# Six edits to the order of stores, norms and loads in a fused forward and backward kernel: last stores from SyncE, a store behind the first norm's power steps, norms by groups and behind sums, an own tile for a gradient, a table loaded later

## The chip, the core and the metric

The kernel runs on one core of a Trainium2 chip. The core has TensorE (PE) for matrix products, VectorE (DVE), ScalarE (ACT) and GpSimd (POOL) for elementwise work, SyncE (SP), which here does nothing but issue DMA transfers, and 16 DMA engines, which carry the transfers that SP and POOL issue. The five engines run their own instruction streams and meet only at semaphores. The metric is the device time of one execution in microseconds. The kernel before takes 729.11 us, the median of 3 runs (725.36 to 734.2).

## What is computed

A residual stack of four parts over x = A_q, of shape [1, 2048, 448] in bf16: two gated long convolutions (A) and two SiLU MLPs (B), each behind a layernorm without weights; the same weights serve both layers. Both the output and the gradients of seven of the inputs come back.

```python
def _A_ref(q, k, v, shift_k, ssm_k, ssm_D):
    k_shift = sum(k_pad[:, t:t + S, :] * shift_k[:, ks - 1 - t] for t in range(ks))
    kv = k_shift * v
    y = irfft(rfft(kv, 2 * S) * rfft(ssm_k, 2 * S))[:, :S]
    return q * (y + kv * ssm_D)

def _B_ref(x, w1, w2):
    return silu(x @ w1) @ w2          # w1 [448, 1792], w2 [1792, 448]

x = A_q
x = x + _A_ref(ln(x), A_k, A_v, A_shift_k, A_ssm_k, A_ssm_D)
x = x + _B_ref(ln(x), B_w1, B_w2)
x = x + _A_ref(ln(x), A_k, A_v, A_shift_k, A_ssm_k, A_ssm_D)
x = x + _B_ref(ln(x), B_w1, B_w2)
out, vjp = jax.vjp(f, A_q, A_k, A_v, A_shift_k, A_ssm_k, A_ssm_D, B_w1, B_w2)
return (out, *vjp(grad_out))
```

(The reference's lines, shortened: the convolution is written with real FFTs of length 4096.)

## The kernel before

The convolution's result y + kv*D does not depend on x, so a first stage (`_ssm_prefix`, about the first 100 us) computes it once for all tokens as Y (`Ysb`), with the FFT written as matrix products; the spectra of ssm_k and kv go to DRAM for the backward part. What is left of part A in the main stage is a norm and a gate, x + ln(x)*Y.

The main stage (`Main.run`) works on the 2048 tokens in four chunks c of 512, each of four tiles `tl` of 128 tokens. All tokens of the residual stream lie in one tile X in SBUF. For each chunk and layer L there are these steps, each a generator whose yields mark where another may come between:

- `T`, `T2`: TensorE transposes of a normed tile, so that the features lie on the partitions (nT). `T2` works by groups of tiles: 0 and 1, then 2, then 3.
- `H`: h = nT times w1 in seven steps; ACT writes silu(h) into aT (L659) and copies h into dT (L664), which `slope` later turns into the slope of silu (L674).
- `O`: aT times w2, eight steps; for each tile DVE adds the result into X (L685, in the waits "X L685"). In layer 1 the output is stored from X by POOL (L687), once a chunk, after tile 3.
- `G`: the gradient times w2 transposed, seven steps, into ghT, which DVE multiplies by the slope (for c = 0 to 3 of layer 1 in the loop at L845). In layer 1 the gradient that goes in is grad_out, which `load_gT` brings in transposed: eight DMA transposes on SP for a chunk, per tile one of 384 features (L750) and one of the last 128 (L751).
- `N`: ghT times w1 transposed, and the backward of the layernorm (`_ln_bwd`, L894 to L899, whose last addition writes its output with the residual gradient added). In layer 1 `_ln_bwd` runs twice a tile, for norm 3 and for norm 2, and both write into X in place; gb is the residual gradient, loaded by SP.
- `_ln` (L250): a layernorm. DVE takes the statistics, adds the epsilon (L268), POOL raises to the power of -1/2 (L270), DVE makes the shift (L272) and, for each tile, the normed n (L277), which POOL stores into N_d for the backward part of A. It takes `groups` of tiles, and each group is one such sequence. The norms are numbered si = 0 to 3. `fwd0(c)` is norm 0, the gate and norm 1; `fwd1(c)` is norm 2, the gate and norm 3.
- `store`: aT or ghT, transposed by SP's DMA transposes into a tile "turned" (L553), goes on to DRAM (a_d, g_d), from where it is loaded for the weight gradients as dstat.

On TensorE the order is written out by hand: `steps` and `weave` take patterns of letters, and each letter runs one generator up to its next yield. The other engines are ordered by a scheduler, under `issue_after` and priorities where the code sets them. Tiles come from pools with a few buffers for a name; a new use of a buffer waits for the last readers of the old one.

The weight gradients (`Jobs`) are products over all tokens, woven in from the last chunk on: the stationary side is dstat, loaded by SP in 512 KB pieces, the moving side is X, grad_out or the normed inputs (L969). `fin_w2` copies a finished block of w2's gradient to SBUF by ACT (L1054) and POOL stores it (L1056).

The last stage (`_ssm_suffix`, from about 508 us) is the backward part of the convolution. It loads the spectra K and KV again in pieces of 2048 columns (`spec_load`, L1150 and L1151), the normed inputs of part A (q_n, L1092), and a table Minvs of 1 MB for the inverse FFT (`_load_minv`, L200), which its products read first at 639 us. POOL issues all of these. The remaining weight gradients fill TensorE between its steps, and the kernel ends with the blocks 12 and 13 of w2's gradient.

Of the kernel before, what the change touches and what calls it, by code (L numbers as in the profile page):

```python
# [17 lines left out]
P = 128  # L18
S = 2048
D = 448  # L20
# [232 lines left out]
def _ln(k, pool, c, src, si, n_g, groups=((0, 4),), pin=False, eng=None, behind=None):  # L253
    nc = k.nc
    for lo, hi in groups:
# [14 lines left out]
        nc.gpsimd.tensor_tensor(out=r[:, lo:hi], in0=ve[:, 0:n], in1=k.mhalf[:, 0:n], op=ALU.pow)  # L270
# [7 lines left out]
    if si != 2:  # L278
        lo, hi = groups[0][0], groups[-1][1]
        nc.gpsimd.dma_start(out=_pm(k.N_d[si][:])[:, 4 * c + lo:4 * c + hi, :], in_=n_g[:, lo:hi, :])  # L280
# [243 lines left out]
class Main:  # L524
    def __init__(self, k, es):
# [10 lines left out]
        nc.gpsimd.dma_start(out=_pm(k.Y_d[:]), in_=k.Ysb[:])  # L536
# [61 lines left out]
    def a_fwd(self, c, si, src, n_g, groups, behind=None):  # L598
        nc, X = self.nc, self.X
        if len(groups) > 2:  # L600

            for g in groups:
                _ln(self.k, self.ch, c, src, si, n_g, (g,))
                self.gate(c, src, n_g, (g,))
            return
        _ln(self.k, self.ch, c, src, si, n_g, groups, behind=behind)
        self.gate(c, src, n_g)
# [16 lines left out]
    def fwd0(self, c):  # L624
# [51 lines left out]
    def O(self, c, L, aT):  # L676
        nc, k, X = self.nc, self.k, self.X
        for tl in range(4):
# [7 lines left out]
            if L == 1 and tl == 3:  # L686
                nc.gpsimd.dma_start(out=_pm(k.outs[0][0])[:, 4 * c:4 * c + 4, :], in_=X[:, 4 * c:4 * c + 4, :])  # L687
# [26 lines left out]
    def N(self, c, L, gh, gres, n_b, n_a):  # L714
# [4 lines left out]
        for tl in range(4):  # L719
# [3 lines left out]
            Gt = self.X[:, t, :] if L == 1 else g1[:, tl % 2, :]  # L723
            pn = k.psum.tile([P, 512], FP32, name="ps_n", tag="po", bufs=2)
# [6 lines left out]
            _ln_bwd(k, self.ch, u0[:], n_b[:, tl, :], cp[:, tl, :], gres(tl), Gt)  # L731
            if L == 1:
                nc.vector.tensor_tensor(out=gyt[:, tl, :], in0=Gt, in1=n_a[:, tl, :], op=ALU.mult)
                u1 = self.t([P, D], "lb_u1", "lb_u0", 3)
                nc.vector.scalar_tensor_tensor(out=u1[:], in0=Gt, scalar=k.rstd[2][:, t:t + 1], in1=self.Y[:, t, :], op0=ALU.mult, op1=ALU.mult, accum_out=cp[:, 4 + tl, 0:1])
                self.chain = _ln_bwd(k, self.ch, u1[:], n_a[:, tl, :], cp[:, 4 + tl, :], Gt, Gt)
# [32 lines left out]
    def run(self, es):  # L769
# [19 lines left out]
        with tc.high_priority():  # L789
            self.fwd0(0)  # L790
        nT = self.nT()
# [7 lines left out]
        steps("GGGtttt", G=g20, t=self.T2(self.n0[0][1], nT))  # L799
# [20 lines left out]
        for c in range(4):  # L820
# [6 lines left out]
            o = self.O(c, 1, aT2)  # L827
            if c == 0:
                weave("O" * 8, O=o)
            else:  # L830
# [5 lines left out]
                if c == 1:  # L836
                    weave("OOOOOGGOGGOTOT", O=o, G=g, T=self.T(self.n0[c + 1][1], nT))
                elif c < 3:
                    weave("OOOOOGOGGOGGGGTOT", O=o, G=g, T=self.T(self.n0[c + 1][1], nT))
                else:  # L840
                    jobs.start()
                    weave("OOOOOGOGGOGGGGO", O=o, G=g)
# [59 lines left out]
class Jobs:  # L902
# [148 lines left out]
    def fin_w2(self, ft, ps):  # L1051
        nc, k = self.nc, self.k
        o = self.out()
        nc.scalar.copy(o[:], ps[:, :D])  # L1054
        self.flush()
        nc.gpsimd.dma_start(out=k.outs[8][ft * P:(ft + 1) * P, :], in_=o[:])  # L1056
# [57 lines left out]
def _ssm_suffix(k):  # L1114
# [9 lines left out]
    with ExitStack() as es:  # L1124
# [11 lines left out]
        _load_minv(k, nc.gpsimd)  # L1136
        with ExitStack() as e1:
# [8 lines left out]
            def spec_load(cp):  # L1146
# [4 lines left out]
                nc.gpsimd.dma_start(out=kk[:, 1, :], in_=k.SPEC_d["KV"][:, lo:hi])  # L1151
# [178 lines left out]
```

## Time and the profile before

| | us |
|---|---|
| median of 3 runs | 729.11 (725.36 to 734.2) |
| the profiled execution | 729.0 |
| its span, first to last instruction | 727.2 |
| PE, busy | 685.5 |
| DVE, busy | 489.0 |
| ACT, busy | 444.3 |
| POOL, busy | 126.4 |

The profiled execution is one run of the program, recorded by the hardware profiler; its mean granted TensorE clock was 0.996 of full speed. A line of the timeline has the start in us, the duration in us (of all the instructions that it groups), the engine, the line of code, the operation, the names of what it writes and reads with their sizes, and in brackets how long the engine had been idle and what released it. "issue" as a releaser means that the profile shows nothing that the engine waited for. SPq and POOLq are the instructions by which SP and POOL issue DMA transfers; the time of such a row is the issue's, and the landing comes later: the rows "DMA to landing us" have the time from issue to landing, smallest, median and largest.

### The profile page before, as it was taken

The page shows a single profiled execution, that of the slowest core. Times are in us where ns is not written, and L with a number is a line of the kernel's source. Part 1 is how long each engine was busy: PE and PEld are TensorE (multiplying, and loading weights), DVE is VectorE, ACT ScalarE, POOL GpSimd, SP SyncE. Part 2 cuts the span into 40 slices and gives each one's busy share as a digit, 9 for nine tenths or more (in the row PEclk, how much of TensorE's full clock was granted, in tenths as well). Part 3 has the DMA queues.
Part 4 walks back from the last instruction along what each step waited for, and adds up shares of the span by engine and source line. Part 5 has one row for each costly group of instructions (what it writes and reads, how often), then busy time and mean ns, then how long its engine had stood idle before and what let it go on. Part 6 is the DMA issues. An engine that isn't in the chain of part 4 may idle for free.

```text
span 727.2 us, 12726 instructions
## 1 busy us (share of the span) xinstructions
PE 685.5 (94%) x4933; PEld 377.5 (52%) x4976; DVE 489.0 (67%) x1157; ACT 444.3 (61%) x585; POOL 126.4 (17%) x213
## 2 busy tenths in 40 slices
PE   5997889998989999999999999999899999999996
PEld 4986644434444444444444444545466666656553
DVE  4789865656897747976379534825168768859760
ACT  4887877686777868779687783132755555454200
POOL 1134410201011100111001000000312323244220
PEclk9999999999999999999999999999999999999999
DMA  9949799899989999499985997199998798789860
GB/s 315 292 141 289 249 298 135 126 264 248 211 202 243 220 240 242 109 228 262 186 200 130 244 244 299 30 222 218 369 411 298 251 337 288 244 307 357 314 210 20
DMA packets 195581, 172.59 MB, mean 237 GB/s; under 512 B 142882, under 2 KB 173730, under 8 KB 194368
## 3 DMA queue, kind: packets, MB, share of 16 engines
q1 hardware_dynamic: 180992, 115.73, 63.1%
q0 software_dynamic: 14064, 56.04, 22.2%
q8 instruction: 39, 0.64, 0.4%
q14 instruction: 22, 0.18, 0.1%
q10 hardware_dynamic: 464, 0.00, 0.0%
HBM read 73.25 MB, written 60.10 MB: 183 GB/s over the span
## 4 chain that ended last, share of the span: by engine, by line
PE 59%; issue 10%; DVE 6%; DMA 3%; ACT 3%; POOL 2%; SPq 1%; POOLq 0%; DVEq 0%
PE ps_d L969 12%; PE ps_g L499 10%; PE ps_n L726 10%; PE ps_h L499 9%; PE ps_o L681 8%; PE ps_d L1004 2%; DMA dstat<-a_d 2%; PE ps_v L228 2%; PE ps_v L227 2%; PE ps_t L567 1%; DMA out_dram<-X 1%; DVE B1v L1276 1%; PE ps_tr L1158 1%; ACT dT L674 1%; DVE gka L1277 1%
## 5 line engine op out<-in xcount | busy, mean ns | idle before, releaser
L969 PEld LDWEIGHTS <-dstat 128*128 128x128 bf16 x800 | 75.5, 98 | 69.0 <-DMA dstat<-a_d 4.0
L499 PE MATMUL ps_h<-nT,w1sb 128*128 128x512 bf16 (+1 forms) x434 | 95.9, 380 | 5.6 <-ACT dT L664 2.2
L681 PE MATMUL ps_o<-w2sb,aT 128*128 128x448 bf16 x448 | 88.8, 352 | 4.0 <-DVE X L685 4.0
L726 PE MATMUL ps_n<-w1T,ghT 128*128 128x448 bf16 x448 | 92.1, 352 | 0.1
L499 PE MATMUL ps_g<-nT,w2T 128*128 128x512 bf16 (+1 forms) x378 | 81.1, 380 | 1.1 <-issue 0.5
L709 ACT CAST ghT<-ps_g 128x512 bf16<-128x512 f32 (+1 forms) x74 | 54.1, 761 | 42.4 <-PE ps_g L499 42.2
L659 ACT ACTIVATE aT<-ps_h 128x512 bf16<-128x512 f32 (+1 forms) x82 | 59.9, 758 | 29.9 <-PE ps_h L499 27.4
L499 PEld LDWEIGHTS <-w1sb 128*128 128x128 bf16 (+1 forms) x448 | 35.5, 97 | 61.7 <-issue 27.7
L681 PEld LDWEIGHTS <-aT 128*128 128x128 bf16 x448 | 43.5, 98 | 44.5 <-issue 4.5
L726 PEld LDWEIGHTS <-ghT 128*128 128x128 bf16 x448 | 43.3, 98 | 41.0 <-DVE ghT L711 1.4
L499 PEld LDWEIGHTS <-w2T 128*128 128x128 bf16 (+1 forms) x448 | 35.3, 97 | 55.3 <-issue 20.9
L894 DVE SCALAR_TENSOR_TENSOR lb_v<-lb_u,n 128x448 bf16<-128x448 bf16 x48 | 29.9, 623 | 42.9 <-ACT lb_u L730 42.4
L270 POOL TENSOR_TENSOR rstd<-ln_ve,mhalf 128x2 f32<-128x2 f32 (+2 forms) x27 | 23.8, 881 | 193.7 <-DVE ln_ve L268 193.7
L674 ACT ACTIVATE dT<-dT 128x1024 bf16<-128x1024 bf16 (+1 forms) x64 | 55.0, 937 | 0.1
L969 PE MATMUL ps_d<-n3m,dstat 128*128 128x448 bf16 x224 | 48.6, 352 | 0.2
L969 PE MATMUL ps_d<-n1m,dstat 128*128 128x448 bf16 x224 | 48.6, 352 | 0.1
L227 PE MATMUL ps_v<-Gsb,pa 128*128 128x128 bf16 x336 | 44.2, 223 | 2.7 <-DVE pa L456 2.6
L228 PE MATMUL ps_v<-Gsb,pb 128*128 128x128 bf16 x336 | 43.5, 223 | 1.9 <-DVE pb L457 1.9
L664 ACT CAST dT<-ps_h 128x1024 bf16<-128x1024 f32 (+1 forms) x50 | 42.7, 871 | 0.0
L730 ACT ACTIVATE lb_u<-ps_n,rstd 128x448 bf16<-128x448 f32 x32 | 20.7, 647 | 33.2 <-PE ps_n L726 25.4
L969 PE MATMUL ps_d<-go,dstat 128*128 128x448 bf16 x176 | 37.2, 353 | 2.7 <-DMA dstat<-a_d 1.5
L969 PE MATMUL ps_d<-X,dstat 128*128 128x448 bf16 x176 | 37.1, 353 | 1.6 <-DMA dstat<-a_d 1.6
(209 smaller groups left out, 1188.7 us busy)
## 6 DMA issues: line engine op xcount, KB each, us to landing
dstat<-g_d SPq DMA_DIRECT2D x28, 512.0 KB, 5.7
dstat<-a_d SPq DMA_DIRECT2D x26, 512.0 KB, 6.0
a_d<-turned SPq DMA_DIRECT2D x16, 512.0 KB, 3.6
g_d<-turned SPq DMA_DIRECT2D x16, 512.0 KB, 3.3
a_d<-turned SPq DMA_DIRECT2D x16, 384.0 KB, 3.0
g_d<-turned SPq DMA_DIRECT2D x16, 384.0 KB, 3.3
N_d<-n POOLq DMA_DIRECT2D x10, 448.0 KB, 4.1
spec_K<-Z POOLq DMA_DIRECT2D x7, 512.0 KB, 7.1
```

The lines of the kernel that those rows point to most:

```text
L227: nc.tensor.matmul(pv[:, i, :], lhsT=pa[:, i * P:(i + 1) * P], rhs=k.Gsb[:, ga, :], start=True, stop=False)
L228: nc.tensor.matmul(pv[:, i, :], lhsT=pb[:, i * P:(i + 1) * P], rhs=k.Gsb[:, gb, :], start=False, stop=True)
L270: nc.gpsimd.tensor_tensor(out=r[:, lo:hi], in0=ve[:, 0:n], in1=k.mhalf[:, 0:n], op=ALU.pow)
L499: nc.tensor.matmul(ps(u, u + 1)[:, 0, :], lhsT=wT[h, b, ft * P:(ft + 1) * P], rhs=rhs[h, b, :], start=start, stop=stop)
L659: self.last_silu = nc.scalar.activation(aT[hh][:, o:o + hi - lo, :], ps(lo, hi), ACT.Silu)
L664: nc.scalar.copy(self.dpart(dT, 2 * fp + lo, 2 * fp + hi), ps(lo, hi))
L674: self.nc.scalar.activation(d[:, o:o + n, :], d[:, o:o + n, :], ACT.Derivative_silu)
L681: nc.tensor.matmul(po[:, :D], lhsT=aT[ft // 7][:, ft % 7, tl * P:(tl + 1) * P], rhs=self.w2sb[:, ft, :], start=(ft == 0), stop=(ft == NF - 1))
L709: nc.scalar.copy(g, ps(lo, hi))
L726: nc.tensor.matmul(pn[:, :D], lhsT=gh[ft // 7][:, ft % 7, tl * P:(tl + 1) * P], rhs=self.w1T[:, ft, :], start=(ft == 0), stop=(ft == NF - 1))
L894: nc.vector.scalar_tensor_tensor(out=v[:], in0=u0, scalar=-1.0 / D, in1=n_t, op0=ALU.mult, op1=ALU.mult, accum_out=cp[:, 1:2])
L969: self.nc.tensor.matmul(ps[:, :D], lhsT=st[:, t, :], rhs=mov[:, t, :], start=(first and t == 0), stop=(last and t == NT - 1))
```

## The change

1. The stores of the last two blocks (12 and 13) of w2's gradient issue from SyncE instead of GpSimd, and the very last copy out of PSUM is split between ACT (columns 0 to 255) and DVE (256 to 447).
2. The store of Y to DRAM (Y_d, L536) issues after the last power step of the first norm, where it stood ahead of it.
3. At the start of the main stage, the third step of the first G (six matmuls) moves behind the 16 transposes of the normed tile.
4. `fwd1(0)` now goes group by group (tiles 0 and 1, then 2, then 3): norm 2, gate, norm 3 of a group, then the next group. Before, norm 3 came after norm 2 and the gate of all groups.
5. Norm 1 of the next chunk is split off `fwd0` (`fwd0b`) and written down behind the first four O steps.
6. In `N` of layer 1 the gradient between the two `_ln_bwd` has its own tile (gmid), and X is written only by the second. The output store of a chunk goes in two halves of two tiles.
7. `_load_minv` moves from before the spectra's loads to behind the third pair of them.

The order of matmuls on TensorE differs only by point 3. On SP the stream differs in two places: the last two output stores stand at its end, and the last of the eight `load_gT` transposes for chunk 1 (L751, tile 3) stands behind the first transpose of aT (L553) and no longer ahead of it.

```diff
-def _ln(k, pool, c, src, si, n_g, groups=((0, 4),), pin=False, eng=None, behind=None):
+def _ln(k, pool, c, src, si, n_g, groups=((0, 4),), pin=False, eng=None, behind=None, store=()):
...
-        nc.gpsimd.tensor_tensor(out=r[:, lo:hi], in0=ve[:, 0:n], in1=k.mhalf[:, 0:n], op=ALU.pow)
+        k.ln_pow = nc.gpsimd.tensor_tensor(out=r[:, lo:hi], in0=ve[:, 0:n], in1=k.mhalf[:, 0:n], op=ALU.pow)
...
-    if si != 2:
-        lo, hi = groups[0][0], groups[-1][1]
+    if si != 2 and store is not None:
+        lo, hi = store or (groups[0][0], groups[-1][1])
         nc.gpsimd.dma_start(out=_pm(k.N_d[si][:])[:, 4 * c + lo:4 * c + hi, :], in_=n_g[:, lo:hi, :])
...
         nc.sync.dma_start_transpose(out=self.w1T[:], in_=k.B_w1)
-        nc.gpsimd.dma_start(out=_pm(k.Y_d[:]), in_=k.Ysb[:])
...
-        n01 = self.t([P, 4, D], "n01", bufs=2)
-        _ln(k, self.ch, c, self.xs(c), 1, n01)
-        self.n0[c] = (n00, n01)
+        self.n0[c] = (n00, self.t([P, 4, D], "n01", bufs=2))
+
+    def fwd0b(self, c):
+        _ln(self.k, self.ch, c, self.xs(c), 1, self.n0[c][1])
...
-        self.a_fwd(c, 2, self.xs(c), n10, pairs, behind)
-        _ln(self.k, self.ch, c, self.xs(c), 3, n11, pairs)
+        if c:
+            self.a_fwd(c, 2, self.xs(c), n10, pairs, behind)
+            _ln(self.k, self.ch, c, self.xs(c), 3, n11, pairs)
+        else:
+            for g in pairs:
+                _ln(self.k, self.ch, c, self.xs(c), 2, n10, (g,))
+                self.gate(c, self.xs(c), n10, (g,))
+                _ln(self.k, self.ch, c, self.xs(c), 3, n11, (g,), store=(0, 4) if g[1] == 4 else None)
...
-            if L == 1 and tl == 3:
-                nc.gpsimd.dma_start(out=_pm(k.outs[0][0])[:, 4 * c:4 * c + 4, :], in_=X[:, 4 * c:4 * c + 4, :])
+            if L == 1 and tl % 2:
+                nc.gpsimd.dma_start(out=_pm(k.outs[0][0])[:, t - 1:t + 1, :], in_=X[:, t - 1:t + 1, :])
...
             Gt = self.X[:, t, :] if L == 1 else g1[:, tl % 2, :]
+            G1 = self.t([P, D], "gmid")[:] if L == 1 else Gt
...
-            _ln_bwd(k, self.ch, u0[:], n_b[:, tl, :], cp[:, tl, :], gres(tl), Gt)
+            _ln_bwd(k, self.ch, u0[:], n_b[:, tl, :], cp[:, tl, :], gres(tl), G1)
...
-                self.chain = _ln_bwd(k, self.ch, u1[:], n_a[:, tl, :], cp[:, 4 + tl, :], Gt, Gt)
+                self.chain = _ln_bwd(k, self.ch, u1[:], n_a[:, tl, :], cp[:, 4 + tl, :], G1, Gt)
...
             self.fwd0(0)
+        with tc.issue_after(k.ln_pow.ins):
+            nc.gpsimd.dma_start(out=_pm(k.Y_d[:]), in_=k.Ysb[:])
...
-        steps("GGGtttt", G=g20, t=self.T2(self.n0[0][1], nT))
+        steps("GGtttG", G=g20, t=self.T2(self.n0[0][1], nT))
...
             o = self.O(c, 1, aT2)
+            steps("OOOO", O=o)
+            if c < 3:
+                self.fwd0b(c + 1)
             if c == 0:
-                weave("O" * 8, O=o)
+                weave("O" * 4, O=o)
...
-        nc.scalar.copy(o[:], ps[:, :D])
+        if ft == NF - 1:
+            nc.scalar.copy(o[:, 0:256], ps[:, 0:256])
+            nc.vector.tensor_copy(o[:, 256:D], ps[:, 256:D])
+        else:
+            nc.scalar.copy(o[:], ps[:, :D])
         self.flush()
-        nc.gpsimd.dma_start(out=k.outs[8][ft * P:(ft + 1) * P, :], in_=o[:])
+        (nc.gpsimd if ft < NF - 2 else nc.sync).dma_start(out=k.outs[8][ft * P:(ft + 1) * P, :], in_=o[:])
...
-        _load_minv(k, nc.gpsimd)
...
-                nc.gpsimd.dma_start(out=kk[:, 1, :], in_=k.SPEC_d["KV"][:, lo:hi])
+                i = nc.gpsimd.dma_start(out=kk[:, 1, :], in_=k.SPEC_d["KV"][:, lo:hi])
+                if cp == 2:
+                    with tc.issue_after(i.ins):
+                        _load_minv(k, nc.gpsimd)
```

More of the change, by code (lines that the diff above doesn't have):

```diff
@@ L599, in a_fwd @@
         nc, X = self.nc, self.X
[L600 to L605, printed above, removed]
         _ln(self.k, self.ch, c, src, si, n_g, groups, behind=behind)
@@ L730, in N @@
             nc.scalar.activation(u0[:], pn[:, :D], ACT.Identity, scale=k.rstd[2 * L + 1][:, t:t + 1], accum_out=cp[:, tl, 0:1])
[L731 removed]
+            _ln_bwd(k, self.ch, u0[:], n_b[:, tl, :], cp[:, tl, :], gres(tl), G1)
             if L == 1:
[L733 removed]
+                nc.vector.tensor_tensor(out=gyt[:, tl, :], in0=G1, in1=n_a[:, tl, :], op=ALU.mult)
                 u1 = self.t([P, D], "lb_u1", "lb_u0", 3)
[L735 to L736 removed]
+                nc.vector.scalar_tensor_tensor(out=u1[:], in0=G1, scalar=k.rstd[2][:, t:t + 1], in1=self.Y[:, t, :], op0=ALU.mult, op1=ALU.mult, accum_out=cp[:, 4 + tl, 0:1])
+                self.chain = _ln_bwd(k, self.ch, u1[:], n_a[:, tl, :], cp[:, 4 + tl, :], G1, Gt)
             else:
```

6 lines of the change are left out of this document (3 added, 3 removed).

## The prediction

> **What bounds the kernel now.** I read the page first: busy time of each engine, then the chain of work that ended last, then what PE waited for.
>
> ```profile
> span 727.2 us, 12726 instructions
> PE 685.5 (94%) x4933; PEld 377.5 (52%) x4976; DVE 489.0 (67%) x1157; ACT 444.3 (61%) x585; POOL 126.4 (17%) x213
> ...
> PE 59%; issue 10%; DVE 6%; DMA 3%; ACT 3%; POOL 2%; SPq 1%; POOLq 0%; DVEq 0%
> ```
>
> PE is busy for 685.5 of 727.2 us. The change takes no matmul away, so at most 727.2 - 685.5 = 41.7 us are open to it, in all of the program together. What an edit can win is a single idle stretch of PE that it ends, so I looked for those next, in the list of waits and then on the timeline.
>
> ```profile
> PE ps_o L681 <- DVE X L685: 4.0, 2, 2.1
> PE ps_d L969 <- DMA dstat<-a_d: 3.2, 2, 1.6
> ```
>
> The columns are total us, times, longest us. The change has something to do with both of the first, one of the second, and three places more: the first norm, the start of the second layer, and the end, where PE has no work left. Each is short, so the sum is of small terms, made against the profiled execution: 729.0 us, its span of 727.2 and 1.8 around it. That is 0.1 below the 729.11 us median of the three runs (725.36 to 734.2), so no correction is needed.
>
> **The first norm: the Y store behind the powers.**
>
> ```profile
> 102.45 0.17 DVE L268 TENSOR_SCALAR ln_ve<-ln_mv 128x2 f32<-128x2 f32 x1
> 103.09 0.53 POOL L536 DMA_DIRECT2D Y_d<-Ysb  x1 [10.21 <-ACT Ysb L111]
> 103.64 1.39 POOL L270 TENSOR_TENSOR rstd<-ln_ve,mhalf 128x2 f32<-128x2 f32 x2
> 109.63 0.59 PE L499 MATMUL ps_h<-nT,w1sb 128*128 128x512 bf16 x2 [1.63 <-ACT nT L766]
> ```
>
> The second power's input is there at 102.45 + 0.17 = 102.62, and the powers run only from 103.64, behind the store that POOL issues at 103.09. With the store behind them the normed tiles come about 1.0 us earlier (103.64 - 102.62), and PE's wait of 1.63 us at 109.63 shrinks by that: bounds 0.4 and 1.6. The six matmuls of the third G step go behind the transposes; they fill the rest of the wait. Nothing that I find waits for the Y store. But a gain here lasts only until PE next meets something with a fixed time, and it does so 30 us on.
>
> **The second layer's start: groups, and a transpose that changes places.** Its norms now go group by group, so that the first pair's n is not behind the third group's gates. The instruction order on SP changes with it: the last of the eight transposes of grad_out (L751, the last block of 128 columns for the fourth tile) stands behind the first 512 KB transpose of aT (L553), where it stood ahead of it.
>
> ```profile
> 136.45 1.26 SPq L750 DMA_TRANSPOSE nT<-in_grad_out_dram  x1
> 137.76 1.23 SPq L751 DMA_TRANSPOSE nT<-in_grad_out_dram  x1
> 139.11 1.94 SPq L553 DMA_TRANSPOSE turned<-aT  x1
> 139.61 0.87 PE L765 MATMUL ps_t<-ident,n 128*128 128x128 bf16 x8 [1.21 <-DVE n L277]
> 140.32 1.89 PE L499 MATMUL ps_g<-nT,w2T 128*128 128x512 bf16 x8
> DMA to landing us min/median/max: 2.4/2.5/2.6
> DMA to landing us min/median/max: 6.2/6.2/6.2
> DMA to landing us min/median/max: 2.5/4.3/9.7
> 147.08 1.28 ACT L659 ACT_TABLE_LOAD   x1 [0.46 <-DMA turned<-aT]
> 155.19 1.08 ACT L659 ACTIVATE aT<-ps_h 128x512 bf16<-128x512 f32 x2 [0.93 <-DMA turned<-aT]
> ```
>
> The three landing rows are, in order, the two nT transposes here, the aT transpose at 139.11, and all transposes into turned of the whole run. SP issues these back to back (136.45 + 1.26 = 137.71, then 137.76), so their time is set by SP and not by PE's gain further up. Now the quarter lands at 137.76 + 2.5 = 140.26, just ahead of its first reader: the first G product's fourth matmul, at 140.32 + 3/8 of 1.89 = 141.03. In the changed order the aT transpose goes at 137.76 and the quarter at 137.76 + 1.94 + 0.05 = 139.75. If nothing but its issue is late, it lands at 139.75 + 2.5 = 142.25, 1.2 us after the reader's present time; if it lands no sooner than the data ahead of it, at 137.76 + 6.2 = 143.96, 2.9 us after. So the 1.0 us of the first norm and the 1.21 us at 139.61, which no longer needs DVE, both end in a wait for this quarter: worth nothing, and PE comes out 1.2 to 2.9 us later than now. The Trainium skill, on its page "DMA: Bandwidth & Descriptors", section "Queues, rings and completion order", says that on each DMA engine the descriptors of a queue are consumed in ring order; by that rule the later end, 143.96, holds, the sum with nothing given back would be -1.6 instead of -3.5, and the rule speaks against the change. No row of this trace shows two transposes so ordered with a reader waiting for the second.
>
> Some of it comes back: ACT waits 0.46 and 0.93 us for aT's turned buffers at 147.08 and 155.19, at times that SP sets, 1.4 us that PE's chain pays already. From 1.2 nothing is left, from 2.9 there is 1.5. Bounds 0 and +2.9 (if that cover doesn't reach PE); I take **+1.0**, nearer to the later landing with the cover.
>
> **Norm 1 of the next tokens behind four O steps, in the first round.**
>
> ```profile
> 167.48 3.75 PE L681 MATMUL ps_o<-w2sb,aT 128*128 128x448 bf16 x19 [2.13 <-DVE X L685]
> 170.16 0.16 DVE L272 SCALAR_TENSOR_TENSOR ln_nmr<-ln_mv,rstd 128x4 f32<-128x4 f32 x1 [0.94 <-POOL rstd L270]
> 174.87 0.75 DVE L845 TENSOR_TENSOR ghT<-dT,ghT 128x512 bf16<-128x512 bf16 x2
> ```
>
> PE's 2.13 us goes, since the residual sums no longer stand behind that norm on DVE. But DVE has 0.94 us idle in this stretch, and the same work up to the last product at 174.87 + 0.75 = 175.62, which the N matmuls behind O need. PE gets there earlier and waits there instead. Bounds 0 and -0.5 (half of the 0.94 us filled); I take **-0.3**. The full -2.13 would need DVE not to bind, and belongs to a rival. In the later rounds the same split meets no wait of PE in the list: nothing.
>
> **The own tile for the gradient, and the halved store.**
>
> ```profile
> 175.25 0.54 POOL L687 DMA_DIRECT2D out_dram<-X  x1 [1.94 <-DVE X L685]
> 183.85 0.39 DVE L899 TENSOR_TENSOR X<-lb_v,gb 128x448 bf16<-128x448 bf16 x1 [5.18 <-DMA out_dram<-X]
> 194.15 0.24 ACT L730 ACTIVATION_READ_ACCUMULATOR lb_u<-ps_n,rstd 128x1 f32 x1
> 197.09 0.62 DVE L894 SCALAR_TENSOR_TENSOR lb_v<-lb_u,n 128x448 bf16<-128x448 bf16 x1
> 203.28 0.92 PE L681 MATMUL ps_o<-w2sb,aT 128*128 128x448 bf16 x4 [1.90 <-DVE X L685]
> ```
>
> DVE stands 5.18 us, because it may not write X before the output store issued at 175.25 has read it. It is then behind by enough that the fourth tile's chain starts at 197.09, though its input is there at 194.15 + 0.24 = 194.39, and that PE waits 1.90 us at 203.28. With a tile of its own DVE need not wait, the fourth chain starts 2.7 us earlier, and the sum that PE wants comes at about 203.3 - 2.7 = 200.6, before PE's 203.28 - 1.90 = 201.38. **-1.9**; -0.9 if the extra pool tile or the halves of the store cost DVE 1 us at the chain. What is late next is PE itself: behind it I see no DVE wait in this round. For the other three rounds the list has no such wait: nothing.
>
> **The table loaded later.**
>
> ```profile
> 515.98 0.55 POOL L200 DMA_DIRECT2D Minvs<-c_minv  x1 [4.93 <-DMA G_d<-g]
> 525.80 0.53 POOL L1150 DMA_DIRECT2D kk_d<-spec_K  x1 [5.55 <-DMA Minvs<-c_minv]
> 527.00 0.36 PE L969 MATMUL ps_d<-X,dstat 128*128 128x448 bf16 x1 [1.63 <-DMA dstat<-a_d]
> q0 software_dynamic: 141, 0.97, 57.7%
> q1 hardware_dynamic: 139, 0.71, 42.5%
> 558.02 0.54 POOL L1092 DMA_DIRECT2D q_n<-N_d  x1 [4.63 <-DVE lb_v L897]
> 565.69 0.68 DVE L1106 SCALAR_TENSOR_TENSOR q_y<-q_g,rstd,q_y 128x448 bf16<-128x448 bf16 x1
> ```
>
> The two queue rows are of 521 to 525 us: packets, MB, and share of the 16 DMA engines. POOL's queue (q0) has the table in it, and the SP load of dstat that PE waits 1.63 us for at 527.00 gets 42.5%. Without the table the transfers do not stop: the spectrum at 525.80, which waited 5.55 us for it, is issued in its place. So the share hardly rises. Bounds 0 and -1.6; I take **-0.5**. Behind it the table now goes in front of the q loads at 558.02, whose data DVE works on at 565.69: 7.7 us of slack, against 525.80 - 515.98 = 9.8 us that the table took in the busy stretch. It may cost nothing, or the 2.1 us by which the one exceeds the other; PE has other jobs there, so I take nothing.
>
> **The end.**
>
> ```profile
> 715.23 0.53 ACT L1054 CAST dout<-ps_d 128x448 bf16<-128x448 f32 x1 [5.52 <-PE ps_d L969]
> 716.06 0.54 POOL L1056 DMA_DIRECT2D out_dram<-dout  x1 [5.51 <-ACT dout L1054]
> 721.29 0.53 ACT L1054 CAST dout<-ps_d 128x448 bf16<-128x448 f32 x1 [5.52 <-PE ps_d L969]
> 724.01 0.54 POOL L1056 DMA_DIRECT2D out_dram<-dout  x1 [7.41 <-issue]
> DMA to landing us min/median/max: 1.9/4.6/17.1
> ```
>
> The landing row is of all these output stores. The last but one is issued 716.06 - 715.76 = 0.30 us after its copy, the last one 724.01 - 721.82 = 2.19 us after; POOL waits for nothing that the profile shows. It lands at 724.01 + 1.9 = 725.9 at the earliest, with 1.3 us to the end of the span. From SyncE: the halved copy takes 0.30 (0.53 x 256/448) to 0.53, say 0.36; 0.2 to the issue; a landing between the 1.9 here and the 2.5 of a small SP transfer above. The end of the data is 721.29 + 0.36 + 0.2 + (1.9 to 2.5) = 723.8 to 724.4, that is 1.5 to 2.1 earlier: **-1.8**, with -1.0 as the near bound if SP too hesitates before its last issue. All of it is on the path, since nothing runs beside it. The Trainium skill, same page, section "Latency and other measured facts", puts the first byte of an SP-issued transfer at about 600 ns and of a GpSimd one at about 1 us. By that alone the end would gain an estimated 0.4 us and the sum would be -2.1; the 2.19 us row is what I go by.
>
> **The sum:** +1.0 - 0.3 - 1.9 - 0.5 - 1.8 = -3.5, so a span of 723.7 and a time of 725.5 us. All bounds at once the good way: 0 - 0.5 - 1.9 - 1.6 - 2.1 = -6.1 (722.9); the bad way: +2.9 + 0 - 0.9 + 2.1 - 1.0 = +3.1 (732.1).
>
> **Rivals.** *Every wait goes*, and nothing takes its place: 1.63 + 1.21 + 2.13 + 1.90 + 1.63 + 1.9 = 10.4, so 718.6. For it: PE is 94% busy, and each of these waits has its releaser in the diff. Against it: the fixed SP times at 137 to 144 and DVE's full stretch up to 175.62. *Only the end counts*, because each wait of PE inside comes back at the next meeting with DVE or a DMA: -1.8, 727.2. For it: each of the interior gains passes many points where another engine could be last. Against it: after 203 PE rarely waits. *The quarter queues in full* and the cover at 147 and 155 does not reach PE: +2.9 in place of +1.0, 727.4. For it: DVE and PE have slack of their own between 141 and 147, so a late PE need not be what those waits of ACT bound. Against it: the two waits end at SP's times, which the change hardly moves. *The later table stalls DVE at 565*, +2.1: 727.6. *Slower, by one mechanism:* the quarter behind the aT transpose lands as late as the latest transposes into turned, 9.7 us after 137.76, at 147.5; PE then stands 6.4 us at its fourth matmul, and with 1.4 back the term is +5.0 in place of +1.0: +0.5, 729.5. It decides once the landing is past 141.03 + 1.4 + 4.5 = 146.9. Against it: the aT transpose that is nearest landed in 6.2.
>
> **Numbers.** Chances: the forecast 0.45, every wait 0.14, only the end 0.16, the full queue 0.13, the table 0.06, the late landing 0.06. The forecast is the likeliest: 725.5, its own range 722.9 to 728. The range runs from 721.5, which leaves out the case in which every wait goes, to 730.0, which takes in the late landing and leaves out the bounds' far end. About 1% (7.3 us) is what a measurement of this kernel can tell from no change: faster means below 721.8, slower above 736.4. Every wait, and a little of the forecast's lower edge: faster 0.18. No mechanism that I found reaches 736.4; for what I haven't found, slower 0.05. The rest, 0.77, is within 1%.
>
> **What would show it.** In the changed kernel's profile: PE's wait of 1.63 us before its first H matmuls below 0.7; a PE wait of 1 to 4 us on nT loaded from grad_out near 140; no 2.13 us wait for X, and a wait of about that size for ghT or dT near 173 in its place; no DVE wait on the output store, and no 1.90 us; the last copy to the end of span 5.4 us or less in place of 5.9. The prediction is wrong in its main step if PE doesn't wait for that quarter, and wrong on the second if PE starts N early as well.

## The result: 0.48% faster, and the profile after

| | before | changed |
|---|---|---|
| median of 20 runs, us | 729.38 (725.36 to 735.14) | 726.16 (722.53 to 732.04) |
| ratio to before | 1 | 0.9952, 95% interval 0.9933 to 0.9970 |
| profiled execution: span, us | 727.2 | 730.3 |
| its mean granted clock | 0.996 | 0.991 |

0.48% of 729.4 us is 3.5 us, and the forecast's sum was 3.5 us. The total is right; several of its terms are not, and most of what follows is about that. The table also warns the reader: the one profiled execution of the changed kernel is 3.1 us longer than the one of before, while the medians differ the other way. A single profile can't be subtracted from another here. It can be read for which waits are there.

First the page of the changed kernel, then its list of PE's waits (total us, times, longest us):

```profile
span 730.3 us, 12780 instructions
...
PE 695.8 (95%) x4976; PEld 379.4 (52%) x4976; DVE 490.3 (67%) x1158; ACT 444.0 (61%) x585; POOL 126.4 (17%) x215
```

```profile
PE ps_d L975 <- DMA dstat<-a_d: 4.1, 2, 3.5
PE ps_sk L1277 <- issue: 3.2, 1, 3.2
...
PE ps_t L766 <- DVE n L277: 1.9, 1, 1.9
```

The wait for X (4.0 us in two places) is gone. The wait for n is 1.9 us instead of 1.2, the two waits for dstat are 4.1 us instead of 3.2, and a wait that the page calls "issue" has grown from 0.4 us to 3.2. Now SyncE's own rows around the first norms, of the kernel before and then of the changed one, and behind them the changed kernel's PE and DVE rows:

```profile
93.22 25.85 SPq L535 DMA_TRANSPOSE w1T<-in_B_w_dram  x1
119.12 7.39 SPq L785 DMA_DIRECT2D gb<-in_grad_out_dram  x1
126.81 3.17 SPq L750 DMA_TRANSPOSE nT<-in_grad_out_dram  x1
```

```profile
93.18 16.29 SPq L535 DMA_TRANSPOSE w1T<-in_B_w_dram  x1
109.53 3.17 SPq L786 DMA_DIRECT2D gb<-in_grad_out_dram  x1
...
113.01 7.39 SPq L751 DMA_TRANSPOSE nT<-in_grad_out_dram  x1
...
128.24 2.07 SPq L552 DMA_TRANSPOSE turned<-aT  x1
130.35 1.52 SPq L752 DMA_TRANSPOSE nT<-in_grad_out_dram  x1
```

```profile
108.51 0.38 PE L499 MATMUL ps_h<-nT,w1sb 128*128 128x512 bf16 x1 [0.55 <-ACT nT L767]
...
137.56 1.89 PE L499 MATMUL ps_g<-nT,w2T 128*128 128x512 bf16 x8
...
143.43 0.28 PE L766 MATMUL ps_t<-ident,n 128*128 128x128 bf16 x2 [1.92 <-DVE n L277]
...
159.62 10.76 PE L681 MATMUL ps_o<-w2sb,aT 128*128 128x448 bf16 x56
...
173.91 0.36 PE L727 MATMUL ps_n<-w1T,ghT 128*128 128x448 bf16 x1 [0.49 <-DVE ghT L851]
```

```profile
174.30 0.76 DVE L851 TENSOR_TENSOR ghT<-dT,ghT 128x512 bf16<-128x512 bf16 x2
...
177.93 0.39 DVE L905 TENSOR_TENSOR gmid<-lb_v,gb 128x448 bf16<-128x448 bf16 x1
```

What to see: SyncE's transposes of grad_out begin at 113.01, where they began at 126.81. Of these 13.8 us, 9.6 come from the transpose of w1 ahead of them, which took 16.29 us to issue and not 25.85; the rest from the load of gb between them, 3.17 instead of 7.39. The quarter that was expected late is issued at 130.35 and, by its time to landing, is there at 133.3, 4.9 us before its first reader, the fourth matmul of G's first product (137.56 + 3/8 of 1.89 = 138.27). Nothing waits for it. The 56 O matmuls run without a hole, and the last ghT product ends at 175.06, 0.56 us earlier than before (175.62).

The end of the changed kernel, from the POOL, SP, ACT and DVE rows of its last 14 us:

```profile
717.26 0.54 POOL L1066 DMA_DIRECT2D out_dram<-dout  x1 [7.41 <-issue]
...
721.14 6.62 SPq L1066 DMA_DIRECT2D out_dram<-dout  x2
...
726.64 0.37 ACT L1061 CAST dout<-ps_d 128x256 bf16<-128x256 f32 x1 [5.52 <-PE ps_d L975]
...
727.04 0.36 DVE L1062 CAST dout<-ps_d 128x192 bf16<-128x192 f32 x1 [20.13 <-ACT dout L1061]
```

From the start of the last copy to the end of the span: 730.3 - 726.64 = 3.7 us, where it was 727.2 - 721.29 = 5.9. The two halves of that copy do not run side by side: DVE's begins at 727.04, when ACT's is done, and ends at 727.40, so that together they take 0.76 us where the whole copy took 0.53. And a row to keep in mind: POOL's store at 717.26, two stores from the end and here POOL's last, has the same 7.41 us "issue" in front of it that the last store had before.

### The profile page after: what moved, and what is told of

Same layout as the page of the kernel before. It is cut to its first block, busy times and chain, and to the rows that moved or that the text cites. A ratio compares the mean times of both kernels' runs of the same rounds, so it can differ in the third digit from the quotient of the medians.

```text
span 730.3 us, 12780 instructions
## 1 busy us (share of the span) xinstructions
PE 695.8 (95%) x4976; PEld 379.4 (52%) x4976; DVE 490.3 (67%) x1158; ACT 444.0 (61%) x585; POOL 126.4 (17%) x215
## 4 chain that ended last, share of the span: by engine, by line
PE 62%; DVE 8%; issue 5%; DMA 5%; ACT 3%; POOL 1%; POOLq 0%; ACTq 0%; DVEq 0%
PE ps_d L975 14%; PE ps_n L727 11%; PE ps_h L499 10%; PE ps_g L499 10%; PE ps_o L681 8%; PE ps_d L1010 2%; DMA dstat<-a_d 2%; PE ps_t L566 1%; DVE B1v L1288 1%; PE ps_v L228 1%; PE ps_v L227 1%; DVE gka L1289 1%; PE ps_tr L1170 1%; DMA q_y<-Y_d 1%; ACT dT L674 1%
## 5 line engine op out<-in xcount | busy, mean ns | idle before, releaser
L499 PE MATMUL ps_h<-nT,w1sb 128*128 128x512 bf16 (+1 forms) x448 | 98.1, 382 | 2.6 <-ACT dT L664 1.9
L499 PE MATMUL ps_g<-nT,w2T 128*128 128x512 bf16 (+1 forms) x392 | 83.8, 383 | 0.1
L975 PE MATMUL ps_d<-go,dstat 128*128 128x448 bf16 x176 | 39.1, 365 | 3.5 <-DMA dstat<-a_d 3.5
```

Of the source, the lines that this page charges most:

```text
L499: nc.tensor.matmul(ps(u, u + 1)[:, 0, :], lhsT=wT[h, b, ft * P:(ft + 1) * P], rhs=rhs[h, b, :], start=start, stop=stop)
L975: self.nc.tensor.matmul(ps[:, :D], lhsT=st[:, t, :], rhs=mov[:, t, :], start=(first and t == 0), stop=(last and t == NT - 1))
```

## The experiments

Ratios are to the kernel before, run beside each; us beside them are the ratio minus 1, times 730.

**The end alone (e1) and the inner parts alone (e2).** e1 is the kernel before with the changed `fin_w2`; e2 the changed kernel with `fin_w2` and the table as before.

```diff
-        nc.scalar.copy(o[:], ps[:, :D])
+        if ft == NF - 1:
+            nc.scalar.copy(o[:, 0:256], ps[:, 0:256])
+            nc.vector.tensor_copy(o[:, 256:D], ps[:, 256:D])
+        else:
+            nc.scalar.copy(o[:], ps[:, :D])
         self.flush()
-        nc.gpsimd.dma_start(out=k.outs[8][ft * P:(ft + 1) * P, :], in_=o[:])
+        (nc.gpsimd if ft < NF - 2 else nc.sync).dma_start(out=k.outs[8][ft * P:(ft + 1) * P, :], in_=o[:])
```

That is e1's edit, on the kernel before. e2 has it the other way round, on the changed kernel, and e3's edit, further down, as well.

> The kernel before with the end alone changed (the last two stores from SyncE, the last copy halved). Theory 1, the forecast's terms: -1.8 us (bounds -1.0 and -2.1), ratio to before about 0.9975, and the last copy's start to the end of the span 4.1 us (bounds 3.8 and 4.9) where it was 5.9. Theory 2, that only the end counts: -3.3 us, the whole of what the change brings. A price of 0.4 us for the issuing engine alone would leave 5.5 us from the last copy to the end.

> Parts 2 to 6 alone (Y store, order of the first G, norms by groups, norm 1 behind the sums, own gradient tile with halved output store); the end and the table as before. Theory 1: -1.2 us (+1.0 - 0.3 - 1.9), ratio about 0.998. Theory 2: PE is some 2 us earlier than in the kernel before at every point from 205 to 510 us, and then stands longer for the weight gradient's dstat loads near 512 and 525, whose landing does not move; from 530 on it is level with before, so 0 us, and the waits for dstat grow from 3.2 us to about 5.

e1: 0.9962 (0.9933 to 0.9991), -2.8 us. e2: 0.9948 (0.9924 to 0.9972), -3.8 us. Together they would be -6.6, more than the whole change brings, so the two overlap. The last two POOL stores of e2 show where:

```profile
713.88 0.54 POOL L1062 DMA_DIRECT2D out_dram<-dout  x1 [3.62 <-ACT dout L1060]
719.92 0.54 POOL L1062 DMA_DIRECT2D out_dram<-dout  x1 [5.50 <-ACT dout L1060]
```

The end's code in e2 is that of the kernel before, but the last store follows its copy at once ("<-ACT dout", not "<-issue"): from PE's last instruction to the end of the span e2 takes 4.1 us, the kernel before 6.0, e1 3.7. So the inner parts alone took 1.9 us off the end.

For "only the end counts", e2 should have come out level; it did not, though 1.9 of its 3.8 us are at the end. PE's second wait for dstat shows that its landing is not at a fixed time either:

```profile
526.11 0.93 PE L969 MATMUL ps_d<-X,dstat 128*128 128x448 bf16 x4 [1.91 <-DMA dstat<-a_d]
```

```profile
523.10 0.93 PE L975 MATMUL ps_d<-X,dstat 128*128 128x448 bf16 x4 [1.98 <-DMA dstat<-a_d]
```

The first row is e1's, the second e2's: as long a wait, 3.0 us earlier, of which 0.9 were there before the main stage began (its first G matmuls start at 103.10 and 102.17). In these two profiles SyncE's loads came earlier with what PE produces ahead of them, and the gain of the inner parts passed.

**The kernel before once more (e5), and the halved output store alone (e8).**

```diff
e8 (on the kernel before)
-            if L == 1 and tl == 3:
-                nc.gpsimd.dma_start(out=_pm(k.outs[0][0])[:, 4 * c:4 * c + 4, :], in_=X[:, 4 * c:4 * c + 4, :])
+            if L == 1 and tl % 2:
+                nc.gpsimd.dma_start(out=_pm(k.outs[0][0])[:, t - 1:t + 1, :], in_=X[:, t - 1:t + 1, :])
```

> The kernel before, profiled a second time. If the 2.19 us between the last copy and its store on POOL belongs to that place of POOL's program, it is there again (1.9 to 2.3 us, idle time named issue, last PE instruction to the end of the span 6.0 us); if it is chance, the store follows its copy by 0.3 us and the end takes 4.1 us. If PE's 1.90 us wait for X near 203 belongs to the order of the code, it is there again; if it hangs on how late the output store lands, it lies between 0 and 2, and grows with DVE's wait for that store (5.18 us before, 2.38 us in the run with only the end changed, which has the same code up to there).

> The kernel before with the output store in halves and nothing else: four more store instructions on POOL far ahead of the end, the end's code as before (POOL issues, whole copy). If POOL's pause belongs to a place in its program, it falls on an earlier store, the last store follows its copy by 0.3 to 0.4 us, the end takes 4.1 us instead of 6.0, and the time falls by about 1.9 us without SyncE. If the pause comes with the last store as such, 6.0 us and no gain there. The halved store may take up to 1.9 us from DVE's wait near 180 as well.

The last POOL store of e5, then the last three of e8:

```profile
727.24 0.54 POOL L1056 DMA_DIRECT2D out_dram<-dout  x1 [7.42 <-issue]
```

```profile
713.88 0.54 POOL L1056 DMA_DIRECT2D out_dram<-dout  x1 [6.69 <-issue]
718.05 0.54 POOL L1056 DMA_DIRECT2D out_dram<-dout  x1 [3.62 <-ACT dout L1054]
724.09 0.54 POOL L1056 DMA_DIRECT2D out_dram<-dout  x1 [5.50 <-ACT dout L1054]
```

e5, one run of 732.2 us: the kernel before pauses at its last store again. With four more stores in POOL's program, hundreds of us earlier, the pause sits two stores ahead of the last, where nothing waits for it, and the end takes 4.1 us (723.18 to 727.3). The pause goes with a place in POOL's program and not with the last store as such. It stands at block 11's store in e2 as well, where two POOL stores follow; in the changed kernel and in e3, e4, e6, e7 and e11 it stands there too, but there block 11's is POOL's last store, so these can't tell a place from a last store. e1, e9 and e10, which issue fewer transfers from POOL than these, show none. It is no fixed count either: counted over POOL's transfers it is the 173rd in the kernel before and e5 and the 175th in the eight others that have it, and e9 and e10, with 173 in all, pass without it.

e8, one line of the change, measured 0.9955 (0.9922 to 0.9988), -3.3 us, which can't be told from the whole change. Its other part is DVE's wait for the output store. Rows of e5, DVE and then PE, and of e1, whose code is the same there:

```profile
182.50 0.39 DVE L899 TENSOR_TENSOR X<-lb_v,gb 128x448 bf16<-128x448 bf16 x1 [5.51 <-DMA out_dram<-X]
...
201.93 0.53 PE L681 MATMUL ps_o<-w2sb,aT 128*128 128x448 bf16 x1 [2.24 <-DVE X L685]
```

```profile
180.14 0.39 DVE L899 TENSOR_TENSOR X<-lb_v,gb 128x448 bf16<-128x448 bf16 x1 [2.38 <-DMA out_dram<-X]
```

```profile
181.52 0.39 DVE L899 TENSOR_TENSOR X<-lb_v,gb 128x448 bf16<-128x448 bf16 x1
```

In three profiles of this code DVE waited 5.18, 5.51 and 2.38 us, and PE, 20 us later, 1.90, 2.24 and nothing. The last row is e8's: no wait, with the gradient written into X in place. The first half of the store is issued 7 us ahead of the second (171.14 and 178.07), and its data is out in time.

**Without the own tile (e7).** The changed kernel with the gradient written into X in place; the halved store stays.

```diff
-            G1 = self.t([P, D], "gmid")[:] if L == 1 else Gt
+            G1 = Gt
```

> The changed kernel with the gradient written into X in place again (no own tile); the output store stays in halves. Theory A, the forecast's term: DVE waits for the store again and PE 1.9 us for X near 200, +1.9 us. Theory B, that the term was a single late landing: DVE waits 1 to 3 us for the first half's landing and PE 0 to 0.5 us, less than 0.5 us at the end.

DVE waits for no store (the same row at 176.12 has no bracket), and PE for no X near 200. Theory B, and less than it allowed: behind a halved store the own tile takes away no wait here at all. The time, 0.9980 (0.9949 to 1.0011), can't be told from the kernel before, nor from the changed kernel, whose interval it overlaps; no row that I found explains a loss, and whether the tile brings something elsewhere stays open.

**The Y store ahead of the powers again (e6).**

```diff
+        nc.gpsimd.dma_start(out=_pm(k.Y_d[:]), in_=k.Ysb[:])
...
-        with tc.issue_after(k.ln_pow.ins):
-            nc.gpsimd.dma_start(out=_pm(k.Y_d[:]), in_=k.Ysb[:])
```

> The changed kernel with the Y store ahead of the first norm's powers, as before; the scheduler then also puts the last transpose of grad_out ahead of the aT transpose again. Theory A, that the Y store set SP's times: the issue of w1T's transpose takes 24 to 26 us again where the changed kernel has 16.3, and the transposes of grad_out begin 7 us later or more; PE waits 1.6 us for nT near 109 where it waits 0.55. Theory B, the forecast's, that SP's times are its own: 16 to 17 us for w1T. For the time both give +0.5 to +1.1 us against the changed kernel.

```profile
92.16 24.76 SPq L535 DMA_TRANSPOSE w1T<-in_B_w_dram  x1
...
124.81 3.22 SPq L752 DMA_TRANSPOSE nT<-in_grad_out_dram  x1
```

Theory A: with the Y store ahead, the issue of w1's transpose takes 24.8 us; over all profiles 24.7 to 26.0 with the store ahead (before, e1, e5, e6, e8) and 16.3 to 16.5 with it behind (the changed kernel, e2, e3, e4, e7, e9, e10, e11). From the start of that transpose to the first transpose of grad_out it is 32.7 to 34.7 us in the former and 19.8 to 26.6 in the latter. On SyncE e6 also has the last transpose of grad_out ahead of the aT transpose again, so it says nothing on that order. The wait before the first H matmuls did not come back: 0.34 us. What hides it is the G step behind the transposes, not the earlier powers: from the first G matmuls of the main stage to these H matmuls it is 6.78 us before and 5.70 in both e6 and the changed kernel. The time, 0.9969 (0.9928 to 1.0009), can't be told from the changed kernel's.

**The table early (e3) and the norms as before (e4).** Each is the changed kernel with that one part undone.

```diff
e3
-                if cp == 2:
-                    with tc.issue_after(i.ins):
-                        _load_minv(k, nc.gpsimd)
...
+        _load_minv(k, nc.gpsimd)
         with ExitStack() as e1:
e4
             for g in pairs:
                 _ln(self.k, self.ch, c, self.xs(c), 2, n10, (g,))
                 self.gate(c, self.xs(c), n10, (g,))
-                _ln(self.k, self.ch, c, self.xs(c), 3, n11, (g,), store=(0, 4) if g[1] == 4 else None)
+            _ln(self.k, self.ch, c, self.xs(c), 3, n11, pairs)
```

> The changed kernel with the table loaded where the kernel before had it. Theory 1: 0.5 us slower than the changed kernel (bounds 0 and 1.6 slower, 2.1 faster). Theory 2: no difference over 0.5 us, since the spectra fill the queue in the table's place and the dstat load that PE needs near 527 lands within 0.5 us of the same time in both.

> The changed kernel with the norms of the second layer's first chunk in the order of before (norm 2 and gate of all groups, then norm 3). Theory 1: PE's wait for the first pair's n at 139 is back, about 1.2 us, and the wait of 1.9 us for the last tile's n near 143 is gone; level at 146 within 0.5 us. Theory 2, that the group order makes the last tile late: PE is 0.7 to 0.9 us earlier at 146 and without the lower clock behind the wait up to 2.4 us; at the end nothing of it is left, since the dstat loads near 512 and 527 take it (within 0.5 us of the changed kernel).

e3: 0.9931 (0.9901 to 0.9961). e4: 0.9935 (0.9909 to 0.9961). Both intervals hold the changed kernel's ratio, so neither part earns anything in time that this can show. In e3's profile PE's waits for dstat are 1.7 and 1.5 us. The first of the two differs from profile to profile, with the table early or late (1.5 to 3.6 us); the second goes with the table: 1.4 to 2.0 us where it is early (before, e1, e2, e3, e8) and 0.7 to 1.1 where it is late (the changed kernel, e4, e6, e10). Left out are e5 and e7, where PE comes 3 us late out of the first wait and has no second, and e9 and e11, which move another load. In e4's the wait for the first pair's n is back, and the one for the last tile is gone:

```profile
138.36 0.82 PE L766 MATMUL ps_t<-ident,n 128*128 128x128 bf16 x7 [1.21 <-DVE n L277]
```

Grouping exchanges 1.2 us there for 1.9 us at 143: the third group's norm 2 stands behind the second group's norm 3 on DVE. From the first G matmuls behind the prefix (102.69 there, 102.81 in the changed kernel, 103.01 in e3) to the same H step near 237 it is 134.2 us in e4, 134.6 in e3 and 136.2 in the changed kernel, whose profile has a fall of the clock in it (last section): 0.4 us for the order of before, and not the 0.7 to 0.9 expected.

**What the remaining waits are (e10, e11), and a version that takes them away (e9).**

```diff
e10, e9
-            nc.gpsimd.dma_start(out=out5v[:, dc, :], in_=gK[:])
+            (nc.scalar if dc < 2 else nc.gpsimd).dma_start(out=out5v[:, dc, :], in_=gK[:])
e11, e9
-            if fts == (5, 6) and i == 1:
-                self.load_n3()
...
             st = self.load(keys[1], ft)
+            if fts == (5, 6) and ft == 6:
+                self.load_n3()
e9
-            for g in pairs:
+            for i, g in enumerate(pairs):
                 _ln(self.k, self.ch, c, self.xs(c), 2, n10, (g,))
                 self.gate(c, self.xs(c), n10, (g,))
-                _ln(self.k, self.ch, c, self.xs(c), 3, n11, (g,), store=(0, 4) if g[1] == 4 else None)
+                if i:
+                    _ln(self.k, self.ch, c, self.xs(c), 3, n11, (pairs[i - 1],), store=None)
+            _ln(self.k, self.ch, c, self.xs(c), 3, n11, (pairs[-1],), store=(0, 4))
```

e9 has e3's edit too.

> The changed kernel with only the first two gK stores moved to ScalarE's queue. If PE's unnamed wait before the first ps_sk matmul (3.2 us in the changed kernel, 0.4 to 3.9 over the runs) is ACT's copy, which stands for a buffer whose store GpSimd issues 7 us after the data is there, then it falls to 0.5 us or less, and the granted clock stays at 1.00 behind it where the changed kernel showed 0.84. If it is something else, it stays between 1 and 4 us.

> The changed kernel with only the n3m load put behind the two dstat loads of 512 KB that follow it. If the ring of SyncE's transfers sets when those land, PE's second wait for dstat (0.7 to 2.0 us near 525) goes to 0 to 0.3, and the first one (1.5 to 3.5 near 512) stays, since its load is ahead of n3m in both. If the shared engines set it, both waits stay.

> The changed kernel with four things more: the table loaded where the kernel before had it; the norms of the first chunk staggered (norm 3 of a group behind norm 2 and gate of the next); the first two gK stores issued by ScalarE, right behind their copies, instead of GpSimd; the 1.8 MB load n3m behind the two dstat loads that it stood between. If the waits add up: PE's wait of 1.9 near 143 to at most 1.2 us, of 0.7 to 2.0 near 525 to at most 0.5, of 1.1 to 3.9 before the first ps_sk matmul to at most 0.5; together some 3 to 5 us under the changed kernel, a ratio of about 0.988 to 0.991 to before. If another transfer is late instead, no wait is shorter and the ratio stays near 0.993 to 0.995.

The unnamed wait before ps_sk was ACT's. ACT's row in the changed kernel, just ahead of it:

```profile
678.84 1.01 ACT L111 CAST gK<-ps_gK 112x1024 bf16<-112x1024 f32 x1 [7.52 <-DMA out_dram<-gK]
```

The copy waits 7.5 us for a buffer whose store POOL issues late, at 666.71, 5.2 us (not the 7 that e10 expected) after its data was there at 661.47, and which lands 12.1 us after that; in e10 ScalarE issues the same store 0.03 us after the data, and it lands in 6.3. PE's bank comes free with the copy's end at 679.85, and PE starts at 680.06. With the stores on ScalarE's queue the wait is gone in e10 and e9; in the eleven profiles without, it is 0.4 us (the kernel before) to 4.0 (e11). In e11 and e9 the second wait for dstat is gone, and the first stays (1.89 and 2.85 us): with the 1.8 MB load no longer between them on SyncE, the second load is in time, wherever the table is. e11 is the clean case of the two; behind a first wait of about 3 us the second was missing in e5 and e7 as well. e10 0.9939 (0.9908 to 0.9970), e11 0.9926 (0.9899 to 0.9953): each alone can't be told from the changed kernel. The clock behind ps_sk, which e10 expected at 1.00, was 0.83 from 670 to 680, behind a wait of 2.10 us for another load. e9, with all four: 0.9884 (0.9848 to 0.9920), 721.3 us, -8.5 us to before and clear of the changed kernel. What is left of its waits there:

```profile
PE ps_d L977 <- DMA dstat<-a_d: 2.8, 1, 2.8
...
PE ps_d L977 <- DMA go<-in_grad_out_dram: 1.0, 1, 1.0
```

No wait for n, none before ps_sk. That staggering the norms ended the wait for n is seen in this profile alone.

## Why the prediction was right in its total, step by step

The terms can be held against PE's way through two stretches: from the first G matmuls of the main stage (102.85 before, 102.81 in the changed kernel) to the O matmuls near 160, and from there to the H step near 240. A star marks a fall of the clock in the stretch, which costs 1.7 us (last section).

| us | before | e5 | e1 | e8 | changed | e2, e3 | e4 | e6 | e7 |
|---|---|---|---|---|---|---|---|---|---|
| first G to O | 57.0 | 56.6 | 55.9 | 59.5* | 56.8* | 55.1 | 54.8 | 56.3 | 56.8* |
| O to H | 81.4 | 83.4* | 80.0 | 79.9 | 79.4 | 79.4 | 79.4 | 79.4 | 79.4 |

**First norm and second layer, +1.0: wrong, in place and sign.** By the prediction's own sign its main step is wrong, since PE doesn't wait for the quarter. The step that failed is "so their time is set by SP and not by PE's gain further up". SyncE's times were not its own: they hung on the Y store, which runs beside w1's transpose, and with that store 1.7 us later (103.09 to 104.83) SyncE was 13.8 us earlier at the transposes of grad_out. The change of places that I priced is there, and costs nothing. In all eight profiles that have it the quarter lands 0.3 to 0.4 us behind the aT data (133.3 and 133.0 in the changed kernel), but 1.1 to 7.0 us before its first reader. That agrees with the Trainium skill's ring order ("DMA: Bandwidth & Descriptors", "Queues, rings and completion order"), by which it should land behind the aT data. In place of the wait for the quarter stood one that I had counted as ended, for the last tile's n. The holes over 0.3 us from 108 to 160 are 1.63 + 1.21 + 0.76 + 0.39 + 0.38 = 4.4 us before and 0.55 + 1.92 + 0.50 = 3.0 after. The waits within H are 0.3 to 0.5 us in the eight profiles with the Y store behind and 0.5 to 2.5 in the five with it ahead; that SyncE's earlier stores shorten them is not shown by itself. Over the first stretch the changed order is 0.7 to 1.9 us ahead of the three profiles of the kernel before (before, e5, e1, whose code is the same there) (55.1 without the fall, against 55.9 to 57.0), where +1.0 was forecast. The first step, too, was not as drawn: the second power, whose input was there at 102.62 before, runs at 104.15, since DVE and POOL now take the first pair's n and its store ahead of it, and the 1.1 us that PE gains there come from the order of the G step (e6).

**Norm 1 behind the sums, -0.3: right.** PE's 2.13 us went, a wait of 0.49 us for ghT came at the place named, not as long as expected, and DVE's last product moved by 0.56 us. In the second stretch 79.4 us stand against the 79.9 of e8, which has the 2.13 us wait but not the X wait near 200: 0.5 us.

**The own tile and the halved store, -1.9: the size holds in two of three profiles, the part does not.** I credited the tile; the halved store does it alone (e8), and the tile adds nothing behind it (e7, 79.4 us). The wait itself depends on when one store lands: 1.90, 2.24 and 0 us at PE in profiles of the same code. In the second stretch it is worth 1.5 us (81.4 against 79.9), and nothing against e1 (80.0), where the store landed early.

**The table, -0.5: seen in the one wait, not in the time.** The second wait for dstat is some 0.8 us shorter with the table late (1.4 to 2.0 us against 0.7 to 1.1), near the -0.5; but e3, with the table early, is no slower. My reason, that the spectra fill the queue in its place, fits POOL's rows; the other cause of that wait, the load ahead on SyncE, is not in the prediction.

**The end, -1.8: size right (5.9 to 3.7 us in the profiles, -2.2), cause wrong.** I took the 2.19 us as the price of a POOL store at the end. It is a pause at a place in POOL's program, which four added stores move away. Against a POOL store without the pause (e2, e8: 4.1 us from PE's last instruction) the issue from SyncE and the halved copy gain 0.4 us together (e1, e3: 3.7). The halves cost 0.2 of that, since they run one after the other (0.76 us for 0.53), where I had counted 0.36. The issue from SyncE gains 0.6: from the end of the copy to the end of the span it is 3.5 us in e2 and e8 and 2.9 in e1 and e3. The estimate of 0.4 us for the issuing engine, from the Trainium skill's first-byte figures ("DMA: Bandwidth & Descriptors", "Latency and other measured facts"), is of that order and somewhat low here.

Read from the rows, the terms are -0.7 to -1.9, -0.5, -1.5 or nothing, and -2.2 at the end: -3.4 to -6.1 in all, by which profile of the old order one takes. The halved store, which the prediction mentioned only as a cost, takes away the X wait and moves the pause by itself; the issue from SyncE takes the pause off the end a second time. That the total came out at 3.5 us is in good part luck: the forecast has the wrong sign on its first term, and it leaves out the wait before ps_sk (0.4 to 4.0 us over the profiles with POOL's stores) and the falls of the clock. The rivals: "every wait goes" fell with the waits for n, dstat and ps_sk; "only the end counts" with e2; the three with a late quarter or a late table with their missing rows.

## What to carry to other kernels

Look at what is under way on the other queues before moving a store: a neighbour there may move by several times as much as the store does, as w1's transpose did here. When an engine pauses with nothing that the profile names, take a second profile and add harmless instructions ahead: if the pause moves in the program, the line under it is not its cause. And undo the parts one by one: of seven parts here, one line alone can't be told from the whole.

## What the runs showed of the hardware

**The clock falls behind waits, not always.** Rows of the windows (5 us from the end of PE's wait for n: busy us and counts by engine, then the granted clock) of the changed kernel and of e3, which wait 1.92 and 1.93 us at this place:

```profile
143.43:148.43 5.00, 5.00 (x19) 2.05 (x20) 0.00 (x0) 2.45 (x4) 0.58 (x1) 0.66 0.99 315
```

```profile
143.64:148.64 5.00, 5.00 (x26) 2.21 (x27) 0.00 (x0) 4.12 (x7) 0.58 (x1) 1.00 0.84 280
```

Over the 13 profiles, beyond the first 20 us: of 7 waits of PE of 3.0 us or more, all were followed by 5 us at a mean clock of 0.50 to 0.71; of 21 between 1.89 and 2.9 us, 8 were; of 17 between 1.45 and 1.8 us, none. But the length of one wait is not the whole of it: eight of the 13 profiles, the changed kernel's and e3's among them, also fall near 68 to 70 us, where the longest waits at hand are 1.1 and 1.3 us. Nearly every fall stands at half the full clock for about 3.4 us (144.0 to 147.4 and 516.0 to 519.4 in the changed kernel), which costs 1.7 us (5 us at 0.66), about as much as the wait. The Trainium skill ("TensorE: Matmul & The Clock Gate", "Part 1: The HAM clock gate") has a monitor with free-running windows of some 3.4 us, which fits the length of a fall and the chance in the middle; but waits far under 3.4 us were enough here. It is the largest difference that I found between profiles of nearly the same code: behind such waits the changed kernel's profile has three falls and e3's none, about 5 of the 8.6 us between their spans of 730.3 and 721.7.

**POOL's pause.** A store issued 2.2 us after its copy, where 0.3 is usual, at one place of POOL's program near the end, alike in the ten profiles that have it; what happens in it the profile doesn't say. In the kernel before no DMA packet moves from 718.5 to 724.0, on the queues that the page names "instruction" either, so no transfer is under way that POOL could be waiting for.

**w1's transpose beside the Y store.** 16.3 to 16.5 us of issue or 24.7 to 26.0, by whether the 1.8 MB store on POOL's queue comes 11.6 us after the transpose's start or 9.9 (104.83 and 103.09 here). Why 1.7 us decide over 9 stays open.
